# Four pairs of a gated projection as seven block products recombined in PSUM, with the work around them moved

## The chip, the cores and the metric

One core of a Trainium2 chip runs the kernel. The metric is the time of one launch on the device, in microseconds; where a kernel ran several times I quote the median. The span that a profile shows is 2.1 to 2.3 us shorter than the launch in most executions; why is not known.

## The reference

The input x is 2048 tokens by 640 features. It is normalised and goes down two branches, whose sum is added to x. One is a state-space layer, the other a gated unit with a spatial product:

```python
z  = gelu(xn @ w_in)                    # 2048 x 640 by 640 x 1728
z1 = z[..., :864]                       # the part that this case is about
z2 = layernorm(z[..., 864:])
g  = einsum('ts,bsf->btf', w_sp, z2) + b_sp     # 2048 x 2048 by 2048 x 864
B  = einsum('bsf,fd->bsd', z1 * g, w_out)

Bu   = xn @ B_bar                       # 640 complex states
h[t] = Lam_bar * h[t-1] + Bu[t]         # a recurrence over 2048 tokens
A    = 2 * Re(h @ C) + xn * Dskip
out  = x + A + B
```

## The kernel before

The kernel is written in bf16 and does its own scheduling. Python code records every operation with the memory that it reads and writes. A list scheduler then orders the operations of each engine with estimated durations, and semaphore waits are made from the recorded intervals. TensorE works in stages: z2, then the state input ("bu"), z1, the spatial product, and the out stage. Meanwhile VectorE does the recurrence and the corrections, and ScalarE evicts PSUM and does the Gelus.

One z1 tile is 128 tokens by 864 columns. A k slice is 128 of the 640 features that are summed over. The tile takes five k slices by two column halves of 432, so ten matmuls that add up in PSUM (`ps` in the rows of the profile, which every matmul of this case writes; the code numbers its banks), then one Gelu and one store to a scratch in DRAM:

```python
def z1_tile(j, half):
    t0 = half * 1024 + j
    b = z_mm(lambda k: xnTv[:, k, t0:t0 + 1017:8], 0, ...)     # 5 x 2 matmuls; every 8th token
    m = z1o_m[nz1[0] % 3]                                      # a ring of three buffers
    act(lambda e: e.activation(m..., ps[:, b:b + 2, 0:FG], ACT.Gelu_apprx_tanh), ...)
    n = 2 * j + half
    dma("sp", z1_d[n], m.ap(FH), [m.iv()], [("z1d", n, n + 1)], ...)
# ...
for j in range(8):
    for half in range(2):
        z1_tile(j, half)
```

The recurrence goes in Horner steps (multiply what is there by a factor, add the next term). Each was three fused multiply-adds on VectorE:

```python
def horner(q, j):
    dve(e.scalar_tensor_tensor(tv, prev, lr, cur, op0=ALU.mult, op1=ALU.add))            # 512, fp32
    dve(e.scalar_tensor_tensor(dst[:, 0:256], prev[:, 256:512], nli, tv[:, 0:256], ...))   # 256
    dve(e.scalar_tensor_tensor(dst[:, 256:512], prev[:, 0:256], li, tv[:, 256:512], ...))  # 256
```

The spatial product already used a seven-product scheme (Strassen's kind): per tile pair, seven products P1 to P7 of eight k slices, where P1 is copied from one PSUM bank to another by ScalarE so that a second product can add onto the copy.

```python
prod(X, "A11", "B11", True, "P1")
act(lambda e: e.copy(pb(Z), pb(X)), ...)           # PSUM to PSUM
prod(Y, "S1", "T1", True, "P5");   ev(f(p5), Y, ...)
prod(X, "S2", "T2", False, "P6");  ev(f(u2), X, ...)
# ... P2, P7, P3, P4
```

## Time and profile before

| what | before |
|---|---|
| median of 3 runs | 261.94 us (261.06 to 262.08) |
| span of the profile | 259.0 us |
| TensorE / VectorE / ScalarE busy | 254.9 / 243.6 / 179.8 us |
| z1 stage: start, length | 80.42, 29.20 us (160 matmuls) |
| spatial stage: start, length | 109.62, 81.76 us (448) |
| out stage: start, length | 191.38, 65.26 us |
| after the start of the last matmul | 2.56 us |

The stages follow from the chain of work that ended last, read in order of time: each piece starts where the one before ended, so a stage's length is the difference of two starts (that of the out stage is from its first matmul's start to the last's).

In the z1 stage TensorE and VectorE are both full, and ScalarE is half idle. What it idles for stands in the row of the z1 Gelus (busy time, mean ns, then the idle time before them and its causes):

```profile
L780 ACT ACTIVATE arena<-ps 128x864 bf16<-128x864 f32 x16 | 14.3, 891 | 13.9 <-PE ps L702 12.5 <-DMA z_scratch<-arena 1.4
```

ScalarE waits for TensorE for 12.5 us and once, for 1.4 us, for a store to free a buffer.

### The profile page before, as it was taken

Reading aid. Unit: us, or ns where it says so; the run is one execution under the profiler, and the core shown is the slowest. Engines: PE = TensorE matmul, PEld = TensorE weight load, DVE = VectorE, ACT = ScalarE, POOL = GpSimd, SP = SyncE. Lnnn points to the kernel's source line nnn. Section 1 sums busy time; section 2 is a strip of 40 time slices with the busy share of each in tenths; the row PEclk is TensorE's granted clock in tenths of the full one; section 3 lists DMA queues with packets and bytes.
Section 4 is the critical chain, followed back from the end, with each engine's and each line's share of the span. In section 5 each row is a group of like instructions: output and inputs, shape, how many; then the busy total and the mean of one; then the engine's idle time right before and its main releaser. Section 6 shows DMA issues by size and latency. Waiting matters only on the chain.

```text
span 259.0 us, 4339 instructions
## 1 busy us (share of the span) xinstructions
PE 254.9 (98%) x1501; PEld 152.1 (59%) x1501; DVE 243.6 (94%) x566; ACT 179.8 (69%) x323; POOL 26.5 (10%) x50
## 2 busy tenths in 40 slices
PE   7999999999999999999999999999999999999996
PEld 3555554444446777755555555555567777777774
DVE  4899999799999999999999999999999999999943
ACT  6899999799986545443333496973979987895110
POOL 3567165211000000000000000000000000000000
PEclk9999999999999999999999999999999999999999
DMA  6947689999205983399999989991232565457621
GB/s 204 311 120 123 141 143 238 235 305 214 62 6 121 210 199 138 117 325 169 235 205 166 246 196 194 224 216 52 54 130 79 141 172 131 103 142 215 147 78 54
DMA packets 90324, 42.49 MB, mean 164 GB/s; under 512 B 73054, under 2 KB 90302, under 8 KB 90302
## 3 DMA queue, kind: packets, MB, share of 16 engines
q1 hardware_dynamic: 89982, 42.09, 67.8%
q8 instruction: 12, 0.20, 0.3%
q10 hardware_dynamic: 320, 0.12, 0.2%
q14 instruction: 10, 0.08, 0.1%
HBM read 12.28 MB, written 12.45 MB: 95 GB/s over the span
## 4 chain that ended last, share of the span: by engine, by line
PE 92%; DMA 3%; SPq 1%; DVE 1%; POOL 0%; issue 0%
PE ps L1117 32%; PE ps L1265 24%; PE ps L702 18%; PE ps L796 17%; PE ps L1272 2%; DMA arena<-arena 2%; DMA arena<-in_A_x_dram 2%; SPq L410 1%; PE ps L723 1%; DVE arena L676 0%; DVE arena L644 0%; POOL arena L639 0%; PE ps L660 0%; DVE arena L632 0%; DVE arena L633 0%
## 5 line engine op out<-in xcount | busy, mean ns | idle before, releaser
L1117 PE MATMUL ps<-arena 128*128 128x432 bf16 x448 | 81.9, 346 | 0.0
L1117 PEld LDWEIGHTS ps<-arena 128*128 128x128 bf16 x448 | 43.8, 98 | 37.9
L1265 PE MATMUL ps<-arena 128*128 128x320 bf16 (+2 forms) x456 | 64.5, 296 | 0.0
L1265 PEld LDWEIGHTS ps<-arena 128*128 128x128 bf16 x456 | 44.2, 98 | 17.1
L702 PE MATMUL ps<-arena 128*128 128x432 bf16 x280 | 51.9, 346 | 0.1
L902 ACT ACTIVATE arena<-arena 128x512 bf16<-128x512 bf16 x70 | 46.2, 714 | 1.8 <-DVE arena L906 1.7
L702 PEld LDWEIGHTS ps<-arena 128*128 128x128 bf16 x280 | 34.6, 124 | 16.4 <-DMA arena<-arena 0.5
L796 PE MATMUL ps<-arena 128*128 128x512 bf16 x200 | 43.3, 379 | 0.0
L1130 ACT ACTIVATE arena<-ps,arena 128x432 f32<-128x432 f32 (+1 forms) x32 | 19.8, 620 | 24.7 <-PE ps L1117 24.4
L796 PEld LDWEIGHTS ps<-arena 128*128 128x128 bf16 x200 | 19.6, 98 | 23.5
L825 DVE SCALAR_TENSOR_TENSOR arena<-arena 128x512 f32<-128x512 bf16 x35 | 25.8, 748 | 0.0
L801 ACT CAST arena<-ps 128x512 bf16<-128x512 f32 x40 | 22.1, 602 | 3.7 <-PE ps L796 3.7
L906 DVE TENSOR_TENSOR arena<-arena 128x1024 bf16<-128x1024 bf16 (+1 forms) x42 | 24.5, 599 | 0.0
L780 ACT ACTIVATE arena<-ps 128x864 bf16<-128x864 f32 x16 | 14.3, 891 | 13.9 <-PE ps L702 12.5
L1294 ACT COPY ps<-ps 128x320 f32<-128x320 f32 x24 | 9.9, 412 | 19.3 <-PE ps L1265 19.2
L1286 DVE TENSOR_TENSOR arena<-ps,arena 128x320 bf16<-128x320 f32 (+1 forms) x40 | 18.1, 487 | 5.3 <-PE ps L1272 3.6
L1072 DVE TENSOR_TENSOR arena<-arena 128x1024 bf16<-128x1024 bf16 x32 | 21.2, 687 | 0.5 <-DMA arena<-in_B_w_sp_dram 0.3
L847 DVE TENSOR_TENSOR arena<-arena 128x512 f32<-128x512 f32 (+2 forms) x40 | 21.5, 555 | 0.0
L830 DVE SCALAR_TENSOR_TENSOR arena<-arena 128x256 bf16<-128x256 bf16 (+1 forms) x35 | 16.8, 481 | 0.0
L827 DVE SCALAR_TENSOR_TENSOR arena<-arena 128x256 bf16<-128x256 bf16 (+1 forms) x35 | 16.7, 479 | 0.0
L1232 DVE TENSOR_TENSOR arena<-arena 128x640 bf16<-128x640 bf16 x32 | 14.7, 488 | 0.0
L716 ACT ACTIVATE arena<-arena 128x864 bf16<-128x864 bf16 x12 | 11.1, 921 | 0.0
(117 smaller groups left out, 255.0 us busy)
## 6 DMA issues: line engine op xcount, KB each, us to landing
g_scratch<-arena SPq DMA_DIRECT2D x16, 224.0 KB, 3.0
z_scratch<-arena SPq DMA_DIRECT2D x16, 216.0 KB, 2.4
arena<-z_scratch SPq DMA_DIRECT2D x8, 432.0 KB, 4.3
arena<-in_A_x_dram SPq DMA_DIRECT2D x16, 160.0 KB, 3.6
base_scratch<-arena SPq DMA_DIRECT2D x16, 160.0 KB, 2.2
arena<-base_scratch SPq DMA_DIRECT2D x16, 160.0 KB, 3.0
out_dram<-arena SPq DMA_DIRECT2D x15, 160.0 KB, 2.6
arena<-in_B_w_in_dram SPq DMA_DIRECT2D x8, 216.0 KB, 3.8
```

The lines of the kernel that those rows point to most:

```text
L702: r = e.matmul(ps[:, b + h, 0:FG], lhs(k), winv[:, k, hcol * FH + h * FG:hcol * FH + (h + 1) * FG], start=(k == 0), stop=(k == ND - 1))
L796: r = e.matmul(ps[:, b, :], btv[:, ri, k, q * 128:(q + 1) * 128], xnTv[:, k, tq * 512:(tq + 1) * 512], start=(k == 0), stop=(k == ND - 1))
L801: act(lambda e: e.copy(o[:, ri, tq], ps[:, b, :].rearrange("p (m j) -> p j m", j=8)), [bank(b)], [l_m.iv((q * 8 + j) * 1024 + ri * 512 + t ...
L825: dve(lambda e: e.scalar_tensor_tensor(tv, prev, lr, cur, op0=ALU.mult, op1=ALU.add), pr + [l_iv(q, j)] + cr, [t.iv()], cd(512) + PTR, nm ...
L847: tt = lambda o, a, b, op: (lambda e: e.tensor_tensor(o, a, b, op))
L902: act(lambda e, pv=pv, hv=hv, lo=lo, sc=sc: e.activation(pv, hv[:, lo:lo + 2, 1:257], ACT.Identity, scale=sc), [h.iv(), Civ(cn)], [m.iv((q ...
L906: dve(lambda e, mv=mv, lq=lq: e.tensor_tensor(lq, lq, mv, ALU.add), li + [m.iv(0, 1024 * n)], li, cd(512 * n, 2), "fix%s%d%d" % (nm, q0, j))
L1072: dve(lambda e: e.tensor_tensor(o.ap(1024), x.ap(1024), y.ap(1024), op), [x.iv(), y.iv()] + S_HELD.get(j, []), [o.iv()], cd(1024, 2), "%s_ ...
L1117: r = e.matmul(ps[:, bk, 0:FG], lv_[:, k, :], rv[k], start=(first and k == 0), stop=(k == 7), skip_group_check=True)
L1130: act(lambda e: e.activation(o, pb(bk), ACT.Identity, bias=bias), [bank(bk)] + bi, [dst], ca(FG, psum=True, ptr=1), name)
L1265: r = e.matmul(ps[:, bk, c0:c1], lf(q), rf(q)[:, c0:c1], start=(first and q == 0), stop=(q == 7), skip_group_check=True)
L1286: dve(lambda e: e.tensor_tensor(o[0][:, c0:c1], ps[:, bk, c0:c1], y[0][:, c0:c1], ALU.add), [bank(bk), y[1]], [o[1]], cd(c1 - c0), "%s_%d" ...
```

## The change

The intent is to take an eighth off k slices 1 to 4 in half of the z1 stage. Four of the eight pairs (two token tiles by two column halves) become blocks of 18 matmuls in place of 20: seven products of two slices, plus four matmuls for the fifth slice. The other four pairs are computed as before, and their steps (two matmuls each) are put between the products as fillers. To pay for the block's sums on VectorE, twelve Horner steps give their multiplies to ScalarE. The first product of the second spatial tile is moved forward, and the scheduler's margins are changed. Cut to its core:

```diff
+        def z1_sums():        # once: four sums of tokens (1024), four of weights (864), all on VectorE
+            tt(Sx[0], a(1, 0), a(1, 2), ALU.add, 1024, "ZS1")
+            ...
+            tt(Tx[0], b(0, 1), b(0, 0), ALU.subtract, FH, "ZT1")
+            ...
+        def z1_block(j, stream, order):
+            Z, X, V, Y = 4, 5, 6, 7          # four PSUM banks; the fillers have the other four
+            def P1(): mm(X, A(0, 0), B(0, 0), True, "P1");  cp(Z, X, "p1")     # cp: ScalarE, PSUM to PSUM
+            def P5(): mm(Y, Sv(1), Tv_(1), True, "P5");     act(e.copy(p5, pb(Y)))
+            def P6(): mm(X, Sv(2), Tv_(2), False, "P6");    cp(V, X, "u2")
+            def P2(): mm(Z, A(0, 2), B(2, 0), False, "P2"); k4(Z, 0, 0)
+            def P7(): mm(X, Sv(3), Tv_(3), False, "P7");    cp(W, X, "u3")     # W is Y
+            def P3(): mm(V, Sv(4), B(2, 1), False, "P3");   k4(V, 0, 1);  add(V, "c12")   # add: VectorE
+            def P4():
+                k4(W, 1, 1);  add(W, "c22")
+                mm(X, A(1, 2), Tv_(4), False, "P4");  k4(X, 1, 0)
+                outs(Z, 0, "a");  outs(V, 1, "b")     # two Gelus, two stores
+            # in outs: one column half of both token tiles goes to the scratch
+                dma("sp", z1_d[2 * j:2 * j + 2]...[:, :, c * FG:(c + 1) * FG], mv,
+                    [m.iv()], [("z1d", 2 * j, 2 * j + 2)], ...)
...
+        H_ACT = [(4, j) for j in range(1, 7)] + [(q, j) for j in (2, 4, 6) for q in (2, 3)]
+            if (q, j) in H_ACT:
+                act(... P = lr * prev);  act(... Q[:, 0:256] = nli * prev[:, 256:512])
+                act(... Q[:, 256:512] = li * prev[:, 0:256])
+                dve(dst = cur + P);  dve(dst = dst + Q)          # bf16
+                return
...
-        for j in range(8):
-            for half in range(2):
-                z1_tile(j, half)
+        MID = "P1 P5 1 P6 P2 2 P7 P3 2 P4"                # a number is so many filler steps
+        Z1 = ["4 " + MID] + ["5 " + MID] * 2 + ["5 " + MID + " 1"]
+        for j, order in enumerate(Z1):
+            z1_block(j, stream, order)
...
-            spatial(j, (0, 1, 2) if j % 2 == 0 else (3, 4, 5))
+            spatial(j, BK[j % 2], mid=(lambda: spatial(1, BK[1], only_p1=True)) if j == 0 else None)
```

Left out are the scheduler's margins, priorities, and the later place of some constants.

## The prediction

> **What bounds the kernel now.** I read the page's first part, then the chain that ended last, then that chain in order of time, then the waits of TensorE alone. The page's first part and the two lines of its fourth part:
>
> ```profile
> PE 254.9 (98%) x1501; PEld 152.1 (59%) x1501; DVE 243.6 (94%) x566; ACT 179.8 (69%) x323; POOL 26.5 (10%) x50
> ...
> PE 92%; DMA 3%; SPq 1%; DVE 1%; POOL 0%; issue 0%
> PE ps L1117 32%; PE ps L1265 24%; PE ps L702 18%; PE ps L796 17%; PE ps L1272 2%; DMA arena<-arena 2%; DMA arena<-in_A_x_dram 2%; SPq L410 1%; PE ps L723 1%; DVE arena L676 0%; DVE arena L644 0%; POOL arena L639 0%; PE ps L660 0%; DVE arena L632 0%; DVE arena L633 0%
> ```
>
> The chain is 92% matmuls. The vector engine has 94% of the span as well, and is the runner-up. In order of time (start, length, who):
>
> ```profile
> 20.66 16.60 PE ps L702 x90
> 37.26 43.17 PE ps L796 x200
> 80.42 29.20 PE ps L702 x160
> 109.62 81.76 PE ps L1117 x448
> 191.38 4.35 PE ps L1265 x32
> ```
>
> From 20.66 us these pieces join without a gap until the last matmul. TensorE's waits in the whole execution are two, both in the first 20 us:
>
> ```profile
> PE ps L530 <- PEq L1526: 0.8, 1, 0.8
> PE ps L660 <- DVE arena L578: 0.7, 2, 0.4
> ```
>
> So from 20.66 us the time is the count of matmuls times their spacing, and nothing but fewer matmuls or a new wait can change it. The piece at stake is the third, the z1 product: 160 matmuls of 432 columns in 29.20 us, 182.5 ns each.
>
> [...]
> - [...]
> - [...] 1024 bf16 elements take 687 ns (L1072), 512 fp32 elements 688 (L847).
> - [...] The trace has 505 ns (L1139).
> - [...]
>
> **The change, part by part.**
>
> *Four z1 pairs by seven products.* A pair is two token tiles by two column halves by five k slices: 20 matmuls. The changed order has, per pair, 7 products of 2 k slices plus 4 matmuls for the fifth slice: 18. The build's instruction order confirms it: 72 matmuls in the new form and 80 in the old, 152 against 160; every other PE group has the same count. Saved: 8 x 182.5 ns = **1.46 us**, all on the bounding chain. A seven-product scheme saves an eighth on products, but here only k slices 1 to 4 take part, and only in half of the pairs: 5% of a stage that is 11% of the span. Weight loads are no obstacle: those of z1 last 143 ns (median of L702) because of their stride, under the 182.5 ns they hide behind; the new sums' tiles have a smaller stride.
>
> *What it adds to the vector engine.* Rows of one group give start-to-end time; the step from one start to the next is about 80 ns shorter, and steps are what fill a queue. Four token sums of 1024 elements on four-of-eight patterns: 1.13 us each at the slow rate (my estimate, twice the step of a 512-element fp32 row), 4.5 us, or 2.4 us if they reach the fast rate. Four weight sums of 864 bf16 at 0.52 us: 2.1 us. Two adds in PSUM per pair, 8 x 0.52 us = 4.2 us (step of L1137). Sum: +10.8 us.
>
> *What it takes from the vector engine.* The twelve late steps were three fused multiply-adds, and become three ScalarE multiplies and two bf16 adds:
>
> ```profile
> L825 DVE SCALAR_TENSOR_TENSOR arena<-arena 128x512 f32<-128x512 bf16 x35 | 25.8, 748 | 0.0
> L830 DVE SCALAR_TENSOR_TENSOR arena<-arena 128x256 bf16<-128x256 bf16 x30 | 14.4, 481 | 0.0
> L827 DVE SCALAR_TENSOR_TENSOR arena<-arena 128x256 bf16<-128x256 bf16 x30 | 14.3, 479 | 0.0
> L906 DVE TENSOR_TENSOR arena<-arena 128x512 bf16<-128x512 bf16 x14 | 5.9, 422 | 0.0
> ```
>
> By steps, 0.66 + 0.40 + 0.40 = 1.46 us leave and 2 x 0.335 = 0.67 us come: -0.79 us, times 12 = -9.4 us. Net for VectorE +1.4 us at most. This move pays for the block, it is not a gain in itself.
>
> *ScalarE* takes on about 0.62 + 0.41 + 0.41 = 1.4 us x 12 = 17 us, and 16 copies of 0.42 us = 7 us. The table of windows shows room: between 80 and 150 us it is busy 31.3 of 70 us. 55 of 70 would still fit, but with less slack per item.
>
> *Second spatial tile's first product moved up; other spacing; constants later.* Only order. No PE wait exists there to remove, so I give them nothing; the early product lengthens the time before the first tile needs its second token sum.
>
> **Rivals.**
>
> *(a) New waits in the blocks.* A block's third product (P6) adds onto the bank that P1 filled, after ScalarE has copied it. Four matmuls stand between, so P6 may start 5 x 182.5 = 912 ns after P1's last matmul starts. The same chain in the spatial stage: last matmul start to copy start 0.38 us, copy 0.50 us, sum 0.88 us, plus some tens of ns for the semaphore. That is just even: 0 to 0.05 us per block if ScalarE is free. At block changes it may not be: after P4 come two Gelus of the pair, one of an ordinary tile, then the next P1's copy, at 0.77 us a step (0.89 less the overlap). From P4's last matmul start: 0.38 + 3 x 0.77 + 0.50 = 3.19 us, where PE gets to the next P6 after 17 x 182.5 ns = 3.10 us. A wait of 0.1 to 0.2 us, up to three times. And the second Gelu needs VectorE's PSUM add; if that queue is late by more than about 0.9 us, the next P5 waits for all of the rest. Spoken for by the tight spacing, against by the author's having set five fillers just there. Cost 0.1 to 0.6 us likely; 2 us or more if VectorE lags in every block.
>
> *(b) VectorE becomes the bound at the end.* The out stage's pair 6 has the tightest link; VectorE's last correction before it, and the first product:
>
> ```profile
> 238.01 0.42 DVE L906 TENSOR_TENSOR arena<-arena 128x512 bf16<-128x512 bf16 x1
> ...
> 240.19 2.06 PE L1265 MATMUL ps<-arena 128*128 128x320 bf16 x14
> ```
>
> Slack 240.19 - 238.43 = 1.76 us. PE arrives 1.46 us sooner and VectorE has 1.4 us more to do: -1.1 us. Against it: VectorE now idles 1.45 us (at 46.7 us, for POOL) and 0.34 us (at 59.5 us), which the sums can fill, and in the changed order one 0.52 us product of the last gate comes after that correction instead of before. That gives back 2.3 us, slack +1.2 us. Should the fills fail, this takes back up to 1.1 us.
>
> *(c) Stores.* The z1 ring keeps three buffers, stores land in 2.4 us (median) and one Gelu already waits 1.4 us for one. New stores have pieces half as long. A Gelu kept waiting now holds up a block, not just itself. Up to 1 us.
>
> *(d) More gain than counted.* Only the first 20 us and the 2.3 us after the last matmul are left; the build's order is unchanged in both, so no.
>
> **Range and chances.** The ceiling is 1.46 us. From it I take 0.3 us for (a), a third of a chance of about 1 us for (b) and (c) together, rounded to 0.3: a net gain near 0.9 to 1.2 us, 0.4%. 261.94 - 1.1 gives 260.8 us. Below: ceiling reached and a run at the low end of before's spread (261.06 - 1.46 = 259.6). Above: blocks wait for VectorE and nothing is gained (262.3). Range 259.8 to 262.2. Faster by over 2% would need 5.2 us, more than three times the ceiling: 1%. Slower by over 2% needs waits of 6.7 us, so all four blocks stuck behind VectorE's queue plus (b): 3%. Within 2%: 96%.
>
> **What would show it.** Right: the z1 matmuls fill 152 x 182.5 ns = 27.7 us instead of 29.2, later stages are the same length and begin 1.1 to 1.5 us earlier; PE waits on ScalarE appear only in z1 and sum to under 0.6 us; VectorE's busy time rises 0 to 1.5 us, ScalarE's 20 to 28 us. Wrong in (a): PE waits on the PSUM-to-PSUM copies or on the add inside the blocks, over 0.3 us each. Wrong in (b): the out stage longer than before's 65.3 us, waiting on L906's successor. Wrong in (c): Gelus waiting for stores to the scratch. The prediction fails if a PE wait of over 2 us shows up anywhere after 20 us, or if the first 20 us change.

At the marks, passages are cut. 1.46 us saved, less 0.3 for (a) and 0.3 for (b) and (c) together, is 0.86, put as 0.9 to 1.2 us.

What the traces of the two kernels give for figures of the prediction that stand there without a row:

- The 505 ns of L1139 are those of a copy of 432 columns from PSUM to PSUM; the next instruction starts 0.42 us after it.
- Token sums: the fast 2.4 us is four times the step of L1072, 0.60 us for 1024 bf16 columns. The slow 1.13 us each is the estimate; the steps of L847 (fp32), 0.335 us at 256 columns and 0.60 at 512, extend to 1.14, and twice the latter is 1.20.
- ScalarE's multiplies: in the kernel before, L902 (512 columns) has a step of 0.61 us. It has no row of 256 columns from SBUF, so the 0.41 us was an estimate; the kernel after has 0.40 (L964, L966). The Gelus' step of 0.77 us is seen there too (L860).
- Weight loads of 128 columns: in the kernel before, those of L702 took 98 ns from contiguous tokens (20.7 to 37 us) and 144 ns from every eighth token (z1), where TensorE was busy without a gap. From the tiles of the new sums they took 112 to 118 ns (L837), and 131 to 139 in the five that came right after a wait.
- The tens of ns for a semaphore are 0.05 us in the chains of the kernel after and of nop1 (the "issue" after a copy).

## More of the kernel before

One view that the prediction used but did not show is needed later, the table of windows for the stretch 87 to 111.6 us. The columns after the length are busy time, with the number of instructions, on TensorE, its weight loads, VectorE, ScalarE and POOL, then clock, DMA share and GB/s:

```profile
87.00:111.60 24.60, 24.60 (x136) 18.87 (x135) 24.60 (x53) 12.07 (x14) 0.13 (x1) 1.00 0.63 173
```

## The result, and the profile after

| | before | after |
|---|---|---|
| median of 4 runs, side by side | 261.81 us (261.06 to 262.08) | 261.18 us (260.74 to 261.30) |
| span | 259.0 us | 258.6 us |
| z1: start, length | 80.42, 29.20 | 80.61, 28.55 |
| spatial: start, length | 109.62, 81.76 | 109.16, 81.76 |
| out: start, length | 191.38, 65.26 | 190.92, 65.26 |
| after the start of the last matmul | 2.56 | 2.55 |

The ratio is 0.9977, with a 95% interval of 0.9953 to 1.0001. A ratio here is the mean time of one kernel's fast runs over that of the other's of the same rounds, so it is not quite the ratio of the medians. The profiled run was the fastest of the four (260.74 us).

The page's first part and the two lines of its fourth, for the kernel after:

```profile
PE 254.3 (98%) x1489; PEld 149.7 (58%) x1493; DVE 243.6 (94%) x570; ACT 201.4 (78%) x375; POOL 26.4 (10%) x50
...
PE 90%; ACT 4%; DMA 3%; issue 1%; DVE 1%; ACTq 0%
PE ps L1268 32%; PE ps L1422 24%; PE ps L930 17%; PE ps L709 7%; PE ps L837 4%; PE ps L730 3%; PE ps L906 3%; DMA arena<-arena 2%; PE ps L1429 2%; ACT arena L860 2%; DMA arena<-in_A_x_dram 1%; ACT ps L846 1%; ACT arena L790 1%; PE ps L667 1%; ACT arena L580 1%
```

VectorE's busy time has not moved at all and ScalarE has 21.6 us more. New on the chain is ScalarE, with 4% of the span. Lines have moved: L837 are the block's matmuls, L906 the fillers, L860 a block's Gelus, L790 the fillers' Gelus, L846 the PSUM copies, L1268 the spatial stage, L1422 the out stage. In order of time, from the chain of the same kernel:

```profile
80.61 1.46 PE ps L906 x8
...
88.06 0.89 ACT arena L860
88.95 0.78 ACT arena L790
89.73 0.43 ACT ps L846
90.17 0.05 issue
90.21 1.10 PE ps L837 x5
...
109.16 81.76 PE ps L1268 x448
190.92 4.35 PE ps L1422 x32
```

What was one line in the kernel before (29.20 us of TensorE) is now broken by ScalarE: two Gelus and a copy must be done before a block's third product may start at 90.21 us. TensorE's waits, in the list of waits for the whole execution, don't show this:

```profile
PE ps L537 <- PEq L1689: 0.8, 1, 0.8
PE ps L730 <- ACT arena L677: 0.5, 1, 0.5
PE ps L709 <- DMA arena<-arena: 0.2, 1, 0.2
```

All three lie before the z1 stage. The semaphores of the blocks are waited for by the weight load that precedes the matmul, so they are in the list for PEld (here between 80 and 110 us):

```profile
PEld ps L837 <- ACT ps L846: 0.9, 3, 0.4
PEld ps L837 <- ACT arena L860: 0.8, 2, 0.5
```

That is 1.7 us of waiting loads, not all of which reaches the matmuls, because a load runs ahead of its matmul (the loads of L837 from 88.72 us, their matmuls from 88.90). What reaches them is read from TensorE's timeline, by the steps between starts:

```profile
89.63 0.53 PE L906 MATMUL ps<-arena 128*128 128x432 bf16 x2
90.21 1.10 PE L837 MATMUL ps<-arena 128*128 128x432 bf16 x5
```

Two matmuls started at 89.63, so the next was due 2 x 0.1825 = 0.365 us later; it came 0.58 us later. The wait is 0.215 us. Without any wait, 152 x 0.1825 = 27.74 us. The stage took 28.55, so its waits sum to 0.81 us, and of the 1.46 us saved 0.65 are left. z1 also began 0.19 us later, which is in the range by which starts differ between profiles (80.26 to 80.91 us by TensorE's own first start, over all profiles of this case but that of noh6). The spatial stage thus starts 0.46 us earlier, and everything after it has its old length.

ScalarE is what changed in the stretch from 87 to 111.6 us, in the table of windows of the kernel after:

```profile
87.00:111.60 24.60, 24.45 (x133) 17.07 (x132) 24.29 (x53) 24.27 (x43) 0.25 (x2) 1.00 0.55 163
```

It went from 12.07 us of 24.60 to 24.27: within z1 ScalarE is full. Whether that is the cause is what the experiments ask. Last, the rows of the added work:

```profile
L963 ACT ACTIVATE arena<-arena 128x512 bf16<-128x512 bf16 x12 | 8.7, 726 | 0.0
L968 DVE TENSOR_TENSOR arena<-arena 128x512 bf16<-128x512 bf16 x12 | 5.0, 417 | 0.0
L851 DVE TENSOR_TENSOR ps<-ps,arena 128x432 f32<-128x432 f32 x8 | 4.8, 610 | 0.0
L813 DVE TENSOR_TENSOR arena<-arena 128x1024 bf16<-128x1024 bf16 x4 | 2.6, 678 | 0.0
```

The token sums (L813) took 678 ns each, the same as the contiguous sums of that size in the spatial stage (L1221, 684 ns). They did reach the fast rate that the prediction held possible (2.4 us) rather than the slow one it counted (4.5 us).

### The profile page after: what moved, and what is told of

It is laid out like the page before. It is cut to its first block, busy times and chain, and to the rows that moved or that the text cites. A ratio compares the mean times of both kernels' runs of the same rounds, so it can differ in the third digit from the quotient of the medians.

```text
span 258.6 us, 4370 instructions
## 1 busy us (share of the span) xinstructions
PE 254.3 (98%) x1489; PEld 149.7 (58%) x1493; DVE 243.6 (94%) x570; ACT 201.4 (78%) x375; POOL 26.4 (10%) x50
## 4 chain that ended last, share of the span: by engine, by line
PE 90%; ACT 4%; DMA 3%; issue 1%; DVE 1%; ACTq 0%
PE ps L1268 32%; PE ps L1422 24%; PE ps L930 17%; PE ps L709 7%; PE ps L837 4%; PE ps L730 3%; PE ps L906 3%; DMA arena<-arena 2%; PE ps L1429 2%; ACT arena L860 2%; DMA arena<-in_A_x_dram 1%; ACT ps L846 1%; ACT arena L790 1%; PE ps L667 1%; ACT arena L580 1%
## 5 line engine op out<-in xcount | busy, mean ns | idle before, releaser
L1268 PE MATMUL ps<-arena 128*128 128x432 bf16 x448 | 81.9, 346 | 0.0
L1268 PEld LDWEIGHTS ps<-arena 128*128 128x128 bf16 x448 | 43.8, 98 | 37.9
L1422 PE MATMUL ps<-arena 128*128 128x320 bf16 (+2 forms) x456 | 64.5, 297 | 0.0
L1422 PEld LDWEIGHTS ps<-arena 128*128 128x128 bf16 x456 | 44.2, 98 | 17.0
L930 PEld LDWEIGHTS ps<-arena 128*128 128x128 bf16 x200 | 19.6, 98 | 23.5
L1281 ACT ACTIVATE arena<-ps,arena 128x432 f32<-128x432 f32 (+1 forms) x32 | 19.6, 617 | 12.8 <-PE ps L1268 12.5
L709 PE MATMUL ps<-arena 128*128 128x432 bf16 x120 | 22.6, 346 | 0.2 <-DMA arena<-arena 0.2
L1221 DVE TENSOR_TENSOR arena<-arena 128x1024 bf16<-128x1024 bf16 x32 | 21.8, 684 | 0.3 <-PE ps L837 0.2
L971 DVE SCALAR_TENSOR_TENSOR arena<-arena 128x512 f32<-128x512 bf16 x23 | 16.9, 742 | 0.7 <-ACT arena L935 0.7
L709 PEld LDWEIGHTS ps<-arena 128*128 128x128 bf16 x120 | 11.5, 98 | 10.3 <-DMA arena<-arena 0.6
L906 PE MATMUL ps<-arena 128*128 128x432 bf16 x80 | 17.4, 346 | 0.0
L837 PE MATMUL ps<-arena 128*128 128x432 bf16 x72 | 16.2, 348 | 0.2
L906 PEld LDWEIGHTS ps<-arena 128*128 128x128 bf16 x80 | 11.5, 144 | 3.3
L837 PEld LDWEIGHTS ps<-arena 128*128 128x128 bf16 x72 | 9.0, 132 | 4.8 <-ACT ps L846 0.9
```

What stands on the lines that cost most here:

```text
L709: r = e.matmul(ps[:, b + h, 0:FG], lhs(k), winv[:, k, hcol * FH + h * FG:hcol * FH + (h + 1) * FG], start=(k == 0), stop=(k == ND - 1))
L837: q = e.matmul(pb(bk), x, y, start=first and i == 0, stop=True, skip_group_check=True)
L906: r = e.matmul(ps[:, bk + h, 0:FG], xnTv[:, k, t0:t0 + 1017:8], winv[:, k, h * FG:(h + 1) * FG], start=(k == 0), stop=(k == ND - 1))
L930: r = e.matmul(ps[:, b, :], btv[:, ri, k, q * 128:(q + 1) * 128], xnTv[:, k, tq * 512:(tq + 1) * 512], start=(k == 0), stop=(k == ND - 1))
L1221: dve(lambda e: e.tensor_tensor(o.ap(1024), x.ap(1024), y.ap(1024), op), [x.iv(), y.iv()] + S_HELD.get(j, []), [o.iv()], cd(1024, 2), "%s_ ...
L1268: r = e.matmul(ps[:, bk, 0:FG], lv_[:, k, :], rv[k], start=(first and k == 0), stop=(k == 7), skip_group_check=True)
```

## The experiments

All kernels gave correct results. Each call ran its own rounds of the kernel before on the same chip; its medians were 261.37 (first two calls), 261.51 and 261.42 us. Each expectation quoted names its theories as they stood then. The theories in short: **placement and stores**, by which the waits come from where the fillers lie (theory 1 in the expectations) and from stores that hold the Gelus (theory 3); **saturation** (theory 2), by which the twelve Horner steps leave ScalarE too little time; and **VectorE at the end**, the prediction's rival (b).

| run | median us | ratio to before (95%) | z1 length us |
|---|---|---|---|
| after2 (the change again) | 261.63 | 1.0005 (0.9984 to 1.0026) | 28.80 |
| after3 (the change again) | 260.88 | 0.9978 (0.9963 to 0.9993) | 29.61 |
| before2 | 261.54 (one run) | | 29.20 |
| respace | 262.58 | 1.0045 (1.0033 to 1.0057) | 28.72 |
| ring6 | 265.93 | 1.0161 (1.0139 to 1.0184) | 28.66 |
| ring6s | 262.74 | 1.0041 (1.0023 to 1.0059) | 27.87 |
| noh6 | 262.97 | 1.0083 (1.0050 to 1.0116) | 28.78 |
| noh | 269.56 | 1.0319 (1.0297 to 1.0340) | 29.37 |
| noblk | 261.86 | 1.0020 (1.0004 to 1.0035) | 29.20 |
| nop1 | 261.67 | 1.0012 (0.9999 to 1.0025) | 28.69 |
| best1 | 262.24 | 1.0030 (1.0011 to 1.0048) | 27.74 |
| best2 | 260.24 | 0.9960 (0.9934 to 0.9985) | 27.87 |

### The change again, and the kernel before again: after2, after3, before2

No edit.

> The changed kernel again, for a fair comparison on this chip with more rounds. Both theories: ratio to before 0.996 to 0.999, span 258.3 to 258.9 us, z1 waits of TensorE 0.7 to 0.9 us in the same places (the third product of block 1, the second of blocks 2 and 3).

> The changed kernel a third time, because its first two comparisons with the kernel before differ (0.9977 and 1.0005) by about as much as its effect. By the stages (z1 28.55 and 28.80 us in place of 29.20, the spatial and out stages unchanged) the gain should be 0.4 to 0.65 us: ratio 0.9975 to 0.9985. Over 1.000 again: something before the z1 stage costs it time. Waits in z1 0.7 to 1.1 us, in the same places as before.

> The kernel before, profiled once more, to see how much the first 37 us vary without any change: in the first profile the state-input product began at 37.09 us, in the changed kernel and four variants at 37.5 to 39.8 us. If that is chance (when transposed loads land), 37.1 to 37.8 us here; if the change causes it, 37.0 to 37.2 us.

The three comparisons of the change with the kernel before give -0.6, +0.3 and -0.5 us in medians. The gain is small and differs from round to round; two of the three intervals include 1. The z1 stage took 28.55, 28.80 and 29.61 us in the three profiles, 28.99 on average, so its waits were 0.81, 1.06 and 1.87 us. (The profile of after3 is of its slowest run, 263.08 us, and that of the first comparison of its fastest, so these two are near the ends of what the kernel does.) The kernel before had 29.20 us both times, to the hundredth.

So after2 missed its expectation: ratio, span (259.2 us) and waits all lie above the ranges. In after3 the ratio was as expected and the waits, 1.87 us, were not. Part of after2's slowness lies outside the span: three of its six launches were 2.9 to 3.8 us longer than their spans, where those of the kernel before are 2.1 to 2.3. By the medians of the spans the change was faster both times, 258.85 against 259.2 us in after2 and 258.7 against 259.3 in after3. before2 answered its question: its z1 began at 80.48 us in place of 80.26, and its state-input product at about 37.3 in place of 37.09 (its first record is missing), so starts shift without any change, but by less than those of most variants.

By the steps between TensorE's starts, the waits have a constant and a varying part. Each profile has 0.21 us at the third product of the second block, 0.27 at the second product of the fourth, and small ones that bring this part to 0.67 us in each. What varies are the first two products of the third block: 0.13, 0.39 and 1.20 us. The chain of after2 shows what they hang on:

```profile
89.10 2.64 DMA z_scratch<-arena
91.74 0.02 issue
91.75 3.71 DMA z_scratch<-arena
95.46 0.02 issue
95.49 0.02 ACT arena L860
```

A block's first store goes out at 89.10 and lands at 91.74. Its second store is issued only then (at 91.75), and the code has a reason: both stores are recorded as writing the same interval of the scratch (`("z1d", 2 * j, 2 * j + 2)` in the diff), although they write different column halves. It lands at 95.46, and only then has the second block's Gelu a buffer of the ring of three to write. In all three profiles that Gelu began 0.02 us after this store's landing (94.80, 95.46 and 96.03 us). That Gelu and the one after it hold the four PSUM banks that the third block's first two products need. Counted from the start of the z1 piece in the chain, this Gelu began after 14.21 us in the first profile (94.82 - 80.61), 14.46 in after2 (95.49 - 81.03) and 15.27 in after3 (96.05 - 80.78). The steps between these, 0.25 and 0.81 us, are those by which the third block's waits grew, 0.26 and 0.81 us. What differs between the profiles is the second store's own time from issue to landing, 3.36, 3.71 and 4.66 us; its issue did not come later (10.8, 10.7 and 10.6 us after the start of z1). This is the prediction's rival (c), in a form that it had not seen: a wait of one store for another.

### Fillers elsewhere, the ring as it was: respace

```diff
-        Z1 = ["4 " + MID] + ["5 " + MID] * 2 + ["5 " + MID + " 1"]
+        Z1 = ["2 P1 P5 1 P6 1 P2 1 P7 1 P3 P4",       "5 P1 P5 2 P6 2 P2 P7 2 P3 P4",
+              "6 P1 P5 2 P6 1 P2 1 P7 P3 3 P4",       "4 P1 2 P5 P6 P2 2 P7 2 P3 P4"]
```

> The changed kernel with the same seven products, the same twelve ScalarE steps and the same 152 z1 matmuls; only the places of the 40 ordinary steps between the products differ. Theory 1 (the 0.8 us of z1 waits come from where the fillers stand: bursts of Gelus and copies in ScalarE's queue right where TensorE needs a copy): the waits go, the z1 stage falls from 28.55 us to 27.7 to 27.9 us, the span is 0.6 to 0.8 us under the changed kernel's. Theory 2 (ScalarE is full from 87 to 111 us, so work has to be taken away from it): waits only move, z1 stays at 28.3 us or more and the span within 0.3 us of the changed kernel's.

z1 took 28.72 us, no better than the change, and in the range of theory 2. The wait at the second block's third product is gone, but the third block waits 0.48 us for its second product, and ScalarE's list of waits has

```profile
ACT arena L860 <- DMA z_scratch<-arena: 1.9, 2, 1.1
```

The blocks' Gelus are held by stores twice, for 0.8 us before the third block's second product and for 1.1 us at 115.7 us, where an eviction of the spatial stage comes late behind it and TensorE loses 0.37 us (that stage took 82.14 us). Moving fillers alone does not help while the stores bind.

### A longer ring: ring6, and ring6s with other places too

```diff
+        z1r_m = z1o_m + [Mem(bt_m.lo + 1728 * k, 1728) for k in range(3)]   # in the dead B matrices
-            m = z1o_m[nz1[0] % 3]
+            m = z1r_m[nz1[0] % len(z1r_m)]
```

ring6s also moves the fillers ("4 P1 1 P5 1 P6 P2 2 P7 1 P3 1 P4" and so on) and gives the planner 0.05 us more for ScalarE's copies and Gelus and 0.15 us more for the adds in PSUM.

> The changed kernel with six buffers for the z1 Gelu outputs in place of three (three more where the B matrices lay; the loads of C that go there thus come later). Blocks, fillers and ScalarE steps as they were. Theory 3, new after the first runs (a block's Gelus wait for the store that frees their buffer, 0.3 us in the repeat of the changed kernel, 1.9 us in the respaced one, 2.0 us with six steps given back, and the next block's second product waits behind them): no ScalarE wait on the z1 stores is left, TensorE's waits at the second product of blocks 2 and 3 go, those at the third product stay at 0.1 to 0.3 us each; z1 28.1 to 28.5 us. Theory 2 (ScalarE full): z1 stays at 28.5 to 28.8 us.

> Six buffers and the 40 ordinary steps placed anew, with the same ScalarE steps. Theory 1 plus 3 (places of the fillers and the stores, together, are the whole loss): z1 27.8 to 28.1 us, PE waits in it under 0.3 us, span 0.5 to 1.0 us under the changed kernel's on the same chip. Theory 2: z1 stays above 28.3 us.

In ring6 no Gelu waits for a store in z1, and the waits at the second products are gone. Those at the third products stay, at 0.21, 0.35 and 0.22 us, and z1 is 28.66 us. That is longer than theory 3 had it, and in the range of theory 2; so up to here saturation was not refuted. In ring6s both are changed and z1 is 27.87, which is 0.13 from the 27.74 without waits. So there are two limits, one behind the other: three buffers with old or new places 28.55 to 29.61 and 28.72, six buffers with old places 28.66, with new places 27.87. Either cure alone does little; together they recover it. Two reservations: the places in respace and in ring6s are not the same, and ring6s also has other margins in the planner, so this is not a clean square.

Both kernels are slower as a whole, and ring6s missed its span. The three buffers lie where the C matrices are later loaded: in ring6 five of those loads go out between 109 and 130 us, in the change all ten between 76 and 90. That this makes them slower fits the traces and was not tested by itself. The longest wait in ring6 is in TensorE's list of waits:

```profile
PE ps L1269 <- DVE arena L1222: 2.1, 1, 2.1
```

L1222 are VectorE's sums of w_sp. They stood behind a gate product that started at 132.07 us, just after a store of an earlier gate (issued at 129.03) had landed at 131.99. The spatial stage was 85.68 us in place of 81.76, and the wait is not all of it: by the steps between starts the wait is 2.26 us, and after it ten matmuls came about 0.36 us apart in place of 0.1825, in a stretch (133.3 to 136.8 us) where the granted clock was 0.51. That is another 1.65 us. In noh, by contrast, the clock was 1.00 after a wait of 2.85 us; why it fell here is not shown. In ring6s the stage was 82.27 us.

### Horner steps given back to VectorE: noh6 and noh

```diff
-        H_ACT = [(4, j) for j in range(1, 7)] + [(q, j) for j in (2, 4, 6) for q in (2, 3)]
+        H_ACT = [(4, j) for j in range(1, 7)]      # noh6; in noh: H_ACT = []
```

> The changed kernel with the six ScalarE steps of the parts 2 and 3 (about 8.5 us of ScalarE, most of it in the z1 stage) given back to VectorE (about 4.7 us). Theory 1: waits in z1 stay at 0.4 to 0.9 us, since the fillers stand where they stood. Theory 2: waits in z1 fall under 0.2 us. Both: VectorE's slack before the out stage's products, 1.75 us at its tightest, is used up, and TensorE waits there for 1.5 to 3 us in all; ratio to before 1.000 to 1.008.

> The changed kernel with all twelve steps back on VectorE (9.4 us more there by the prediction's sum). The prediction had it that this move only pays for the blocks: VectorE's slack of 1.75 us before the out stage is overdrawn by 7.7 us or more, TensorE waits 6 to 9 us there in all, ratio 1.02 to 1.035. If VectorE has more slack than that view shows: under 4 us of waits, ratio under 1.015. z1 waits by theory 1 and 3 stay at 0.4 us or more.

With six steps given back ScalarE is busy 16.30 of the 24.60 us from 87 us on, and with all twelve 16.67. The row of noh6:

```profile
87.00:111.60 24.60, 24.31 (x132) 17.37 (x130) 24.20 (x49) 16.30 (x26) 0.25 (x2) 1.00 0.52 144
```

If saturation were the cause, the waits should fall. z1 took 28.78 and 29.37 us, within the range of the change itself, with waits of 1.04 and 1.63 us (theory 1 had 0.4 to 0.9 for noh6). **This speaks against saturation**, but it is not a clean test, because VectorE got the work: before the fourth block the third block's Gelus now waited 1.6 us in both for VectorE's add in PSUM, which no Gelu did in the change. In the change those Gelus stood behind ScalarE's own Horner multiplies: they began at 102.11 us, though the block's last matmul had started at 101.22. The 2.7 us later start of z1 in the profile of noh6 (82.96 us) belongs to the slowest of its runs (265.44 us). It is there before z1 and before the state input, from 23.36 us on (20.66 in the kernel before), and is not explained.

These two also measure what the twelve steps are for. The page's busy time of VectorE rises from 243.6 to 247.8 and 252.4 us, and TensorE now waits in the out stage. In noh, TensorE's list of waits for its matmuls has

```profile
PE ps L1422 <- DVE arena L1052: 6.7, 5, 2.7
```

By the steps between starts the waits from the first product of the out stage on sum to 7.7 us. The prediction had 9.4 us for twelve steps on VectorE and 1.76 us of slack at the end: 9.4 - 1.76 = 7.6. With six steps, 4.7 - 1.76 = 2.9 us at most; the out stage grew by 1.95 us (67.21). So without the transfer to ScalarE the blocks cost more than they save, and its size was right.

### Everything but the blocks: noblk

```diff
-        z1_sums()
...
+        for j in range(8):
+            for half in range(2):
+                z1_tile(j, half)
```

> The changed kernel with the old z1 loop (160 matmuls, no sums), everything else of the change kept, VectorE thus about 10 us lighter. If the blocks alone make the difference, as the prediction has it: z1 29.2 us without a wait, span within 0.2 us of before's, ratio 0.999 to 1.001. If the later constants, the other spacing or the ScalarE steps do something of their own, span 0.4 us or more away from before's.

z1 is 29.20 us without a wait, as before. The time is 0.5 us above the kernel before (ratio 1.0020). Of this, 0.17 us is a wait near the end of the spatial stage (at 187.46 us); the rest is a later start of z1 and I have no cause for it. By the expectation's own measure this is its second case (the medians of the spans are 259.7 and 259.2 us). So the other parts of the change gain nothing by themselves, and in these rounds they cost about 0.5 us.

### The second spatial tile's first product back in its place: nop1

```diff
-            spatial(j, BK[j % 2], mid=(lambda: spatial(1, BK[1], only_p1=True)) if j == 0 else None)
+            spatial(j, BK[j % 2])
```

> The changed kernel with the second spatial tile's first product back in its own place. The prediction gave this move nothing. In the changed kernel's trace the copy of the first spatial tile's first product ends at 112.16 us, because the last Gelus of z1 stand ahead of it in ScalarE's queue, and that tile's third product would come up at 111.92 us without the move. If that is right: TensorE waits 0.2 to 0.8 us in the first tile, spatial stage 82.0 to 82.6 us in place of 81.76. If the prediction is right: no wait, 81.76 us.

The chain of nop1 shows a wait that the change does not have:

```profile
111.90 0.43 ACT ps L1285
112.33 0.05 issue
112.38 79.01 PE ps L1268 x432
```

L1285 is the copy of the spatial stage's own P1. It stands behind the last z1 Gelus in ScalarE's queue, and the third product of that tile waits 0.30 us for it. The spatial stage is 82.07 us in place of 81.76. The move thus is worth 0.3 us in this kernel, where ScalarE is full at the end of z1. The prediction gave it nothing, because the kernel before had no wait there; the kernel after would have had one. In whole times the two cannot be told apart (ratios 1.0012 against 0.9977 to 1.0005).

### Versions meant to be better: best1 and best2

best1 is ring6s with places and Horner steps found by a random search with the kernel's own planner, which was given the longer durations. best2 keeps the change's Horner steps and adds only one buffer, placed where two of the ten C loads are delayed rather than five:

```diff
+        z1r_m = z1o_m + [Mem(bt_m.hi - 1728, 1728)]
+                if op.name.startswith("z1st") and s.name.startswith("gelu1"):
+                    at += 1.5                    # the planner expects stores to land later
-        Z1 = ["4 " + MID] + ["5 " + MID] * 2 + ["5 " + MID + " 1"]
+        Z1 = ["2 P1 2 P5 2 P6 1 P2 P7 P3 3 P4",   "5 P1 P5 1 P6 1 P2 1 P7 P3 1 P4",
+              "4 P1 2 P5 P6 P2 1 P7 P3 3 P4",     "6 P1 2 P5 P6 1 P2 1 P7 P3 1 P4"]
```

> Six buffers, steps placed anew, and six of the twelve ScalarE steps chosen in other parts and steps so that fewer meet a block's Gelus; VectorE's total unchanged. All theories: z1 27.7 to 28.0 us. If waits at the start of the blocks remain above 0.3 us in all, something else than buffers, fillers and ScalarE steps makes them (the PSUM adds of VectorE).

> Four buffers for the z1 Gelus (one more, at the end of where the B matrices lay, so that only two loads of C come late and not five), the 40 ordinary steps placed anew with the store's landing planned 1.5 us later, the twelve ScalarE steps as in the change. If the z1 waits come from the stores and the filler places together, and the later slowness of the six-buffer kernels from the late loads of C: z1 27.8 to 28.2 us, PE waits after z1 under 0.2 us, time 0.3 to 1.0 us under before's (ratio 0.996 to 0.999). If only late loads were avoided and the stores still bind: z1 28.4 us or more.

best1 has no wait in z1 (27.74 us), but 0.26 us in the spatial stage, where a sum came late behind a store (82.03 us), a later start of z1 and a tail of 2.94 us. It is slower than the kernel before. best2 has, by its chain,

```profile
80.50 0.73 PE ps L909 x4
...
108.37 81.76 PE ps L1271 x448
190.13 4.35 PE ps L1425 x32
```

and in the whole execution one wait of TensorE:

```profile
PE ps L539 <- PEq L1694: 0.8, 1, 0.8
```

z1 is 27.87 us (108.37 - 80.50), the spatial stage 81.76. Against the kernel before it saves 1.27 us in medians (0.9960, interval 0.9934 to 0.9985), near the 1.33 us by which z1 got shorter and a little more than the 0.3 to 1.0 expected. ScalarE is as full as in the change, 24.00 of 24.60 us from 87 us on:

```profile
87.00:111.60 24.60, 24.60 (x136) 17.45 (x135) 23.86 (x50) 24.00 (x42) 0.25 (x2) 1.00 0.56 163
```

A full ScalarE and a z1 stage with 0.13 us of waits go together here, as they do in ring6s (24.23 us busy). **Saturation by itself thus falls as the cause**, and by this more than by noh6. best2 is the fastest kernel measured here, but it did not run in the same rounds as the change, so how much it gains over the change is not measured.

The plain cure, recording the two column halves of the scratch apart so that the second store need not wait, was not run. That the stores hold the Gelus is shown by their landings and by the longer ring. That the false dependence is what makes the store late is read from the code and from three traces, not tested by itself.

## Why the prediction was right or wrong

The time, 261.18 us, is 0.4 us above the predicted 260.8 and within the range; it is within 2% of the kernel before, as given the large chance. That says little for the mechanism: the range also held the median of the kernel before, 261.81 us, so a change without any gain would have fallen into it as well. By the prediction's own signs the account was half right: z1 took 28.55 us and not 27.7, its waits were 0.81 us and not under 0.6, and later stages began 0.46 us sooner and not 1.1 to 1.5.

**The saving: right.** The block and filler matmuls run at their spacing; best1 took 27.74 us for 152 of them, which is the ceiling of 1.46 us. The later stages kept their length.

**Rival (a), waits in the blocks: mechanism right, mis-sized.** The arithmetic of 3.19 against 3.10 us, so a wait of 0.1 to 0.2 us at a block change, is met by the 0.215 us seen at 90.21, with the very chain described: two Gelus of the pair, one of a filler, then the copy. By the trace it took 3.31 us, from 86.90 to 90.21. But the 0.3 us taken for (a) was to cover all blocks. The constant part of the waits measured 0.67 us, about double, just over the upper end of the "0.1 to 0.6 us likely". Its largest piece, 0.29 us with the step after it, at the fourth block's second product, is not in the prediction's sum: there the Gelus came late behind Horner multiplies that the change had moved to ScalarE. This is what the averaging of ScalarE hid: 55 of 70 us over two stages left out that within z1 it would be full. Fullness by itself is not the cause, as best2 shows; that it leaves a queue little room to catch up after a late item is argued, not measured.

**Rival (c), stores: named, but weighed too lightly.** It was given a third of a chance of about 1 us, jointly with (b). It is in all three profiles of the change, with 0.13, 0.39 and 1.20 us, 0.6 on average, and it is the part of the z1 stage that differs from profile to profile. I had looked at the size of the pieces of the stores, and not at the fact that a pair's two stores are made to follow each other. That a late item in ScalarE's queue held up what stood behind it is seen here: in after3 ScalarE idled 1.12 us before the Gelu at 96.05, with the copies of the next block behind it. Averaged over the three profiles z1 is 28.99 us, a gain of 0.21 us in place of the 0.9 to 1.2 expected, and the three pairs of medians average to a gain of 0.3 us. The two measures agree on the size, small as it is beside the differences from run to run.

**Rival (b), VectorE at the end: right that it would not come.** The slack before the out stage's pair 6 is 239.73 - 237.97 = 1.76 us after, and was 1.76 us before. TensorE came to it only 0.46 us sooner, but best2, where it came 1.25 us sooner (the out stage at 190.13 in place of 191.38), has no wait there either. VectorE's busy time is unchanged, where up to 1.4 us more was allowed; the token sums were cheaper than counted (2.6 us by row in place of 4.5). noh shows that the slack and the worth of a Horner step were sized rightly.

**ScalarE: right** within the named 20 to 28 us (21.6). **The early product: wrong by 0.3 us**, as the one profile of nop1 shows.

Left open: why z1 starts up to 0.65 us apart (2.7 us in noh6) between profiles and why the tail is 2.55 to 3.25 us, which together are as large as the gain; and why noblk is slower than the kernel before by more than its one wait.

## What to carry to other kernels

Work moved to an engine with idle time must be checked against that engine's load in the very stage where it lands, and against its queue's order: before the change ScalarE waited for TensorE (12.5 us before the z1 Gelus), after it TensorE's loads waited for ScalarE (1.7 us), though TensorE stayed the bounding engine with nearly the same busy time (254.9 and 254.3 us). When a tile is split into pieces that are stored separately, follow the dependences that are recorded for the stores: two writes to different parts of one interval became here a chain of two DMA latencies (2.64 and 3.71 us in after2), and the ring of buffers passed it on to the compute (0.13, 0.39 and 1.20 us of TensorE's waits). If one cure for a wait changes nothing, look for a second limit just behind it before dropping the cure.
